# One PSUM pair or two single banks for the VectorE share of the softmax exponential

## The chip, the core and the metric

The kernel runs on one core of one Trainium2 chip. The metric is the device time of one execution in microseconds (us). Five engines work side by side, each with its own queue of instructions in a fixed order: TensorE (PE in the profile; PEld is its weight loading), VectorE (DVE), ScalarE (ACT), GpSimd (POOL) and SyncE (SP, which here only issues DMAs). They meet through semaphores. TensorE writes its products to PSUM, which has eight banks of 512 float32 columns on 128 partitions.

## The reference

```python
xn = layernorm(x)                                   # x: 2048 x 640
q, k, v = split(xn @ wqkv)                          # 32 heads of 20 columns
p = softmax(q @ k.T / sqrt(20))                     # 32 heads, 2048 x 2048 each
s = (p @ v, heads side by side) @ wo
u = gelu(layernorm(xn).T @ w1 + b1)                 # mixes over tokens: 640 x 1536
g = silu((u @ w2 + b2).T)
out = x + s * g
```

The scores are 32 x 2048 x 2048 numbers, and every one goes through an exponential. That is most of the element-wise work of the kernel.

## The kernel before, in words

**Units.** The scores are cut into 2048 units of 128 keys x 512 queries, one PSUM bank each. A unit is one head `g` of a group `G` of four heads, one stretch `p` of 512 queries and one block `c` of 128 keys. The 64 units of one `G` and one `p` make a pass; there are 32 passes. A unit's score product contracts over 32 rows only (20 of them used), so four of them, one for each head of the group, fit side by side in the array (`emit_st`, L910). After the exponential the unit is multiplied with v (`emit_pv`, L1015), which adds up all units of a pass in one accumulator bank, 6. At the end of a pass VectorE reads that bank out and normalises it (`ep_steps`: transpose L1036, reciprocal L1042, product L1047, transpose back L1049), which marks the passes in a trace.

**Two engines take exponentials.** ScalarE owns two pairs of banks, `ACT_GROUPS = ((0, 1), (2, 3))`, and does a pair with one `activation` of 128 x 1024 (L935), in turn. VectorE owns one pair, `DVE_GROUPS = ((4, 5),)`. It has no exponential and makes one out of six steps over the bits of the score (`start_dchain`, N is 512 times the banks in the group):

```python
(tensor_scalar(w3, lo, 0x7FFF, None, ALU.bitwise_and), ...)          # L974, reads PSUM
(tensor_scalar(v_, w_, 1.0 / 256.0, -128.0, ALU.mult, ALU.add), ...) # L975
(tensor_scalar(l_, w_, a3 / 65536.0, ..., ALU.mult, ALU.add), ...)   # L977
(tensor_tensor(l_, v_, l_, ALU.mult), ...)                           # L979
(tensor_tensor(l_, l_, w_, ALU.mult), ...)                           # L980
(scalar_tensor_tensor(o_, zr, ..., l_, ALU.add, ALU.add), ...)       # L981, reads PSUM again
```

The steps need the score on top of a constant, so TensorE first fills each VectorE bank with a product of constants (`prime`, L1313), and the score product is added to it (`start=not dvex` in `emit_st`). A VectorE bank thus goes round: filled with the constant (L1313), score added (L910), L974 to L981, free. The work tiles `ew_sb`, `ev_sb`, `el_sb` exist once; one chain of six runs at a time (`dchain`). The results go to `dpt_sb`, six slots of 512 columns; ScalarE's go to `pt_sb`, 24 slots.

**The order.** All queues are written out beforehand by a planner (`schedule`). It keeps a clock for each engine with prices of its own (VectorE: `dv(n, rate)` = 75 + n x rate ns; ScalarE's pair: 919 ns), and at each step takes the earliest possible candidate, by priority where several are ready. On TensorE a score group for ScalarE has priority 0, v products 1 when many wait, priming 3, a VectorE score group by itself 4; `do_st` puts a primed VectorE group behind a ScalarE group in the same go when its bank is ready. On VectorE a chain step has the lowest priority (90), so other steps stand between those of a chain. No VectorE unit is taken among the last ten units of a pass (`DVE_TAIL_GUARD = 10`, in `dve_room`). On the chip the queues run in this order whatever the true durations are: a TensorE instruction that waits holds all behind it.

**What else runs.** The projections of the next group (L590, evicted by L869 and L865 on VectorE) and the token mixer (L666, evicted by L674; L688 to L704 on VectorE, tanh on ScalarE) are spread over the passes as filler work for TensorE, up to unit 1800 of 2048 (`PACE_TO`). After that come the output projection (L728, L744) and, where the planner wants TensorE busier, products of constants that nobody reads (`warm_step`, L1398); it counts matmul columns in windows of 3413 ns (`_Gate`), a 32-row product as a quarter.

Of the kernel before, what the change touches and what calls it, by code (L numbers as in the profile page):

```python
# [277 lines left out]
class _Kern:  # L278
# [8 lines left out]
    DMAB = 330.0  # L287
    VB = 724
    ACT_GROUPS = ((0, 1), (2, 3))
    DVE_GROUPS = ((4, 5),)  # L290
    ACC_BANK = 6
    DPT = 6
    DVE_EXP = True
# [31 lines left out]
    def build(self):  # L325
# [4 lines left out]
        with es:  # L330
# [4 lines left out]
            def sb(name, shape, d):  # L335
                t[name] = E(nc.sbuf_tensor(name, shape, d))
# [14 lines left out]
            sb("wrm_sb", [P, P + 512], bf)  # L351
            nd = max([len(g) for g in self.DVE_GROUPS] + [0]) * 512 or 2
            sb("ew_sb", [P, nd], u16)
# [26 lines left out]
    def schedule(self):  # L380
# [497 lines left out]
        grp_state = {g: "free" for g in self.ACT_GROUPS}  # L878
        dgrp_state = {g: "free" for g in self.DVE_GROUPS}
        ptr = [0]  # L880
# [337 lines left out]
        act_banks = [b for g in self.ACT_GROUPS for b in g]  # L1218
        dve_banks = [b for g in self.DVE_GROUPS for b in g]
        freebanks.extend([7, 5, 4, 3, 2, 1, 0])  # L1220
# [10 lines left out]
        def fin_bank(b):  # L1231
            return b not in busybanks

        def pe_cands(T):
# [19 lines left out]
            if dveready[0] and self.DVE_EXP:  # L1254
                for dg in self.DVE_GROUPS:
                    if dgrp_state[dg] == "free" and all(fin_bank(b) for b in dg) and nxt[0] + self.DVE_TAIL_GUARD < NU:
# [48 lines left out]
        def dve_room(n):  # L1305
            u0 = nxt[0]
            return (u0 + n <= NU and (u0 % UP) + n <= UP - self.DVE_TAIL_GUARD
                    and all(unit_ok(u0 + i) for i in range(n)))
# [20 lines left out]
        def do_st(grp, us):  # L1329
# [7 lines left out]
            if self.DVE_EXP and dveready[0]:  # L1337
                for dg in self.DVE_GROUPS:
                    if dgrp_state[dg] == "primed" and len(us) + len(dg) <= 4 and dve_room(len(dg)) \
# [152 lines left out]
```

## Time and profile before

| | |
|---|---|
| runs before | 940.67, 945.41, 930.22 us (median 940.67) |
| the profiled execution | 940.67 us, its span 938.9 us |
| busy | TensorE 841.6, VectorE 766.6, ScalarE 866.3 us |
| mean granted TensorE clock | 0.952 |
| ScalarE pairs (L935) | 903, so 1806 of 2048 units |
| VectorE pairs (L974 to L981) | 121, so 242 units |
| VectorE idle before L974 | 118.3 us |
| DMA | 32 GB/s over the span |

The span runs from the first to the last instruction. A row of a group gives the line in the kernel, the engine, output and input tiles with their shapes, the count, the busy time in us and the mean duration of one in ns, then the idle time of that engine just before these instructions and what ended it. The means of ScalarE overlap: one L935 lasts 1064 ns, but 903 of them are busy for 845.6 us, so one starts every 936 ns.

### The profile page before, as it was taken

What the parts mean: (1) busy time and instruction counts of PE and PEld (TensorE: products, weight loads), DVE (VectorE), ACT (ScalarE), POOL (GpSimd) and SP (SyncE); (2) the same over time, 40 slices, a digit from 0 to 9 for tenths busy, and PEclk for the clock granted to TensorE, in tenths of its full rate; (3) what the DMA queues carried; (4) which work ended last, traced back from release to release, by engine and by line L of the source; (5) the groups of instructions that cost most, each with busy time, mean ns of one, the idle gap of its engine ahead of it and who ended that gap; (6) DMA issues with size and microseconds to landing.
All of it is one profiled execution on the core that took longest, in us unless ns stands there. A gap on an engine that the chain in (4) does not pass through costs nothing.

```text
span 938.9 us, 15354 instructions
## 1 busy us (share of the span) xinstructions
PE 841.6 (90%) x5858; PEld 250.5 (27%) x5955; DVE 766.6 (82%) x1255; ACT 866.3 (92%) x942; POOL 13.4 (1%) x31
## 2 busy tenths in 40 slices
PE   6898988998899989889889989989899898899997
PEld 3432222222222222222222222222222223112123
DVE  6878879888878898887888888988888888666577
ACT  2889999999999999999999999999999999878783
POOL 1310000000000000000000000000000000000000
PEclk9999999999999999999999999999999999757569
DMA  8030000000101010100020101101011003400001
GB/s 243 10 97 1 6 7 6 7 6 7 51 1 51 7 51 6 51 7 1 6 74 6 40 8 40 40 2 40 17 30 40 6 7 96 121 1 1 29 29 57
DMA packets 42200, 30.67 MB, mean 33 GB/s; under 512 B 4707, under 2 KB 41571, under 8 KB 42131
## 3 DMA queue, kind: packets, MB, share of 16 engines
q1 hardware_dynamic: 42131, 29.70, 10.6%
q8 instruction: 49, 0.80, 0.4%
q14 instruction: 20, 0.16, 0.1%
HBM read 23.40 MB, written 6.29 MB: 32 GB/s over the span
## 4 chain that ended last, share of the span: by engine, by line
ACT 35%; PE 32%; DVE 25%; issue 4%; DMA 2%; POOL 1%; SPq 0%; DVEq 0%
ACT pt_sb L935 34%; PE ps_all L910 12%; DVE ew_sb L974 7%; PE ps_all L1015 5%; PE ps_all L1313 5%; PE ps_all L666 4%; DVE dpt_sb L981 3%; DVE el_sb L979 3%; PE ps_all L728 3%; DVE el_sb L980 2%; PE ps_all L590 2%; DVE el_sb L977 2%; DVE ev_sb L975 2%; DMA wv_sb<-in_A_wqkv_dram 1%; PE ps_all L609 1%
## 5 line engine op out<-in xcount | busy, mean ns | idle before, releaser
L935 ACT ACTIVATE pt_sb<-ps_all 128x1024 bf16<-128x1024 f32 x903 | 845.6, 1064 | 38.3 <-PE ps_all L910 35.5
L910 PE MATMUL ps_all<-qk_sb 32*128 32x512 bf16 x2048 | 364.6, 400 | 43.5 <-ACT pt_sb L935 32.0
L974 DVE TENSOR_SCALAR ew_sb<-ps_all 128x1024 uint16<-128x1024 uint16 x121 | 148.1, 1224 | 118.3 <-PE ps_all L910 118.2
L910 PEld LDWEIGHTS ps_all<-qk_sb 32*128 32x128 bf16 x2048 | 87.7, 91 | 361.0 <-ACT pt_sb L935 271.0
L1015 PE MATMUL ps_all<-pt_sb,v_sb 128*32 128x512 bf16 x1806 | 169.1, 402 | 0.2 <-ACT pt_sb L935 0.2
L981 DVE SCALAR_TENSOR_TENSOR dpt_sb<-ps_all,el_sb 128x1024 uint16<-128x1024 f32 x121 | 147.8, 1222 | 2.9
L590 PE MATMUL ps_all<-xnT_sb,wqkvp_sb 128*128 128x512 bf16 x289 | 89.5, 386 | 12.3 <-DVE wqk_sb L674 5.6
L979 DVE TENSOR_TENSOR el_sb<-ev_sb,el_sb 128x1024 bf16<-128x1024 bf16 x121 | 83.0, 686 | 2.9
L980 DVE TENSOR_TENSOR el_sb<-el_sb,ew_sb 128x1024 bf16<-128x1024 bf16 x121 | 82.8, 684 | 2.7
L1313 PE MATMUL ps_all<-wrm_sb 128*128 128x512 bf16 x217 | 71.5, 404 | 13.8 <-DVE dpt_sb L981 9.8
L666 PE MATMUL ps_all<-regB,regA 128*128 128x128 bf16 (+1 forms) x369 | 73.9, 299 | 5.6 <-issue 1.7
L666 PE MATMUL ps_all<-regC,regA 128*128 128x512 bf16 (+1 forms) x369 | 71.7, 300 | 4.5 <-DVE qk_sb L869 2.5
L975 DVE TENSOR_SCALAR ev_sb<-ew_sb 128x1024 bf16<-128x1024 uint16 x121 | 50.9, 421 | 3.1
L1015 PEld LDWEIGHTS ps_all<-pt_sb,v_sb 128*32 128x32 bf16 x1806 | 33.7, 95 | 61.9 <-issue 46.7
L977 DVE TENSOR_SCALAR el_sb<-ew_sb 128x1024 bf16<-128x1024 uint16 x121 | 50.2, 415 | 0.0
L1015 PE MATMUL ps_all<-dpt_sb,v_sb 128*32 128x512 bf16 x242 | 49.2, 403 | 0.0
L590 PEld LDWEIGHTS ps_all<-xnT_sb,wqkvp_sb 128*128 128x128 bf16 x320 | 24.1, 97 | 60.4 <-issue 20.8
L609 PE MATMUL ps_all<-wv_sb,xnT_sb 128*128 128x160 bf16 (+1 forms) x160 | 34.5, 313 | 6.4 <-DMA wv_sb<-in_A_wqkv_dram 3.8
L728 PE MATMUL ps_all<-wo_sb,xnT_sb 120*128 120x512 bf16 (+3 forms) x160 | 36.7, 349 | 1.5 <-DVE regC L744 1.3
L666 PEld LDWEIGHTS ps_all<-regB,regA 128*128 128x128 bf16 x384 | 24.8, 97 | 44.1 <-issue 27.7
L666 PEld LDWEIGHTS ps_all<-regC,regA 128*128 128x128 bf16 x384 | 24.8, 97 | 42.8 <-issue 28.6
L869 DVE TENSOR_SCALAR qk_sb<-ps_all,cst_sb 128x512 bf16<-128x512 f32 x32 | 23.7, 742 | 5.7 <-PE ps_all L590 5.3
(69 smaller groups left out, 385.2 us busy)
## 6 DMA issues: line engine op xcount, KB each, us to landing
regA<-in_B_w_dram SPq DMA_DIRECT2D x6, 1024.0 KB, 5.7
regA<-in_B_w_dram SPq DMA_DIRECT2D x8, 768.0 KB
regA<-in_A_x_dram SPq DMA_DIRECT2D x7, 640.0 KB, 4.2
oT_scratch_dram<-stage_sb SPq DMA_DIRECT2D x28, 128.0 KB, 1.8
xnT_sb<-oT_scratch_dram SPq DMA_DIRECT2D x4, 480.0 KB
out_dram<-regC SPq DMA_DIRECT2D x3, 640.0 KB
wqk_sb<-in_A_wqkv_dram SPq DMA_DIRECT2D x2, 800.0 KB
wv_sb<-in_A_wqkv_dram SPq DMA_DIRECT2D x1, 800.0 KB
```

What stands on the lines that cost most here:

```text
L590: steps.append(("pe", lambda e, dc=dc: e.matmul(ps(bk), wqkvp_sb[:, dc, w, G, :], xnT_sb[:, dc, tb * 512:(tb + 1) * 512], start=(dc == 0), ...
L666: steps.append(("pe", lambda e, k=k: e.matmul(ps(bk, n), wap[:, k, col0:col0 + 128], rows[:, k, c0:c0 + n], start=(k == 0), stop=(k == nk ...
L910: pr.pe(lambda e, outp=outp, lhsT=lhsT, rhs=rhs, g=g, dvex=dvex: e.matmul(outp, lhsT, rhs, start=not dvex, stop=True, tile_position=(32 * ...
L935: tk = pr.act(lambda e: e.activation(outp, inp, AF.Exp, scale=math.log(2.0) / 128.0), reads=[bank_slot[b] for b in banks[:n]], writes=[S_( ...
L974: (lambda e: e.tensor_scalar(w3, lo, 0x7FFF, None, ALU.bitwise_and), bs, [S_("ew")], dv(N)),
L975: (lambda e: e.tensor_scalar(v_, w_, 1.0 / 256.0, -128.0, ALU.mult, ALU.add), [S_("ew")], [S_("ev")], dv(N, .26)),
L977: (lambda e: e.tensor_scalar(l_, w_, a3 / 65536.0, (b3 - 64.0 * a3) / 256.0, ALU.mult, ALU.add), [S_("ew")], [S_("el")], dv(N, .26)),
L979: (lambda e: e.tensor_tensor(l_, v_, l_, ALU.mult), [S_("ev"), S_("el")], [S_("el")], dv(N, .52)),
L980: (lambda e: e.tensor_tensor(l_, l_, w_, ALU.mult), [S_("el"), S_("ew")], [S_("el")], dv(N, .52)),
L981: (lambda e: e.scalar_tensor_tensor(o_, zr, -(self.OFFS - 16256.0), l_, ALU.add, ALU.add), bs + [S_("el")], [S_(f"dpt{s0 + i}") for i in r ...
L1015: pr.pe(lambda e, outp=outp, lhsT=lhsT, rhs=rhs, k=k, g=g: e.matmul(outp, lhsT, rhs, start=(k == 0), stop=(k == NB - 1), tile_position=(0, ...
L1313: pe_full(lambda e, b=b: e.matmul(ps(b), wrm_sb[:, 0:P], wrm_sb[:, P:P + 512], start=True, stop=False), [S_("warm"), S_("warm1")], [bank_s ...
```

## The change

One line: VectorE's two banks are no longer a pair but two groups of one bank.

```diff
     ACT_GROUPS = ((0, 1), (2, 3))
-    DVE_GROUPS = ((4, 5),)
+    DVE_GROUPS = ((4,), (5,))
```

Each step of a chain now works on 512 columns instead of 1024, the three work tiles are half as wide, and a chain handles one unit. Each bank is primed and filled by itself, so one can be refilled while the chain of the other runs. The planner lays out all queues anew. Counted in the program that is built: 248 units on VectorE instead of 242 (248 chains of six instead of 121), 900 pairs on ScalarE instead of 903, 248 priming products instead of 242 (nearly all singly, where they stood two by two), 42 products of constants by L1398 instead of 97. VectorE has 2019 instructions instead of 1257. GpSimd's and SyncE's counts are the same. The places of the VectorE units in a pass are typically 0, 1, 8 to 12, 21, 26 to 28, 33 to 35, 40 to 42 and 47 to 49 of 64.

## The prediction

> **What bounds the kernel now.** I read the page's busy shares first, then the costliest groups, then the same groups in the even part of the run, then one chain on the timeline, and last the clock.
>
> ```profile
> PE 841.6 (90%) x5858; PEld 250.5 (27%) x5955; DVE 766.6 (82%) x1255; ACT 866.3 (92%) x942; POOL 13.4 (1%) x31
> L935 ACT ACTIVATE pt_sb<-ps_all 128x1024 bf16<-128x1024 f32 x903 | 845.6, 1064 | 38.3 <-PE ps_all L910 35.5
> L974 DVE TENSOR_SCALAR ew_sb<-ps_all 128x1024 uint16<-128x1024 uint16 x121 | 148.1, 1224 | 118.3 <-PE ps_all L910 118.2
> ```
>
> Three engines are close to full, and ScalarE is fullest. Between 100 and 786 us the group row of L935 says it outright:
>
> ```profile
> L935 ACT ACTIVATE pt_sb<-ps_all 128x1024 bf16<-128x1024 f32 x713 | 664.1, 1068 | 7.9 <-PE ps_all L910 6.0
> ```
>
> ScalarE waits 7.9 us out of 686. There it alone sets the pace, at 0.936 us a pair. VectorE's 118.3 us of idle time before L974 (108 waits on the score product) are the time in which the only pair is primed and filled anew; they cost nothing as long as ScalarE sets the pace. The end of the run is another matter:
>
> ```profile
> PEclk9999999999999999999999999999999999757569
> 84.00:786.00 702.00, 634.74 (x4548) 182.59 (x4627) 595.76 (x922) 692.47 (x757) 0.00 (x0) 1.00 0.07 22
> 808.00:853.00 45.00, 42.00 (x219) 8.77 (x218) 29.78 (x45) 37.20 (x39) 0.00 (x0) 0.62 0.11 34
> 870.00:918.00 48.00, 45.88 (x244) 10.46 (x250) 32.69 (x52) 37.85 (x40) 0.00 (x0) 0.62 0.08 28
> ```
>
> (Columns: stretch, its length, busy us with count of PE, PEld, DVE, ACT, POOL, then granted clock, DMA share, GB/s.) From 808 to 842 and from 859 to 907 us the clock is at half, and TensorE is the full engine. By the marks of L1036, passes 29, 30 and 31 take 32.7, 31.1 and 39.0 us, against 27.1 for the 27 passes before them (731.4 us from 62.1 to 793.5): 21.5 us in all.
>
> **A chain today.** One chain without anything in between:
>
> ```profile
> 319.91 1.23 DVE L974 TENSOR_SCALAR ew_sb<-ps_all 128x1024 uint16<-128x1024 uint16 x1 [0.21 <-PE ps_all L910]
> 321.17 0.43 DVE L975 TENSOR_SCALAR ev_sb<-ew_sb 128x1024 bf16<-128x1024 uint16 x1
> 321.51 0.42 DVE L977 TENSOR_SCALAR el_sb<-ew_sb 128x1024 bf16<-128x1024 uint16 x1
> 321.96 0.69 DVE L979 TENSOR_TENSOR el_sb<-ev_sb,el_sb 128x1024 bf16<-128x1024 bf16 x1
> 322.69 0.69 DVE L980 TENSOR_TENSOR el_sb<-el_sb,ew_sb 128x1024 bf16<-128x1024 bf16 x1
> 323.42 1.22 DVE L981 SCALAR_TENSOR_TENSOR dpt_sb<-ps_all,el_sb 128x1024 uint16<-128x1024 f32 x1
> ```
>
> Starts are 1.26, 0.34, 0.45, 0.73, 0.73 us apart, and L981 lets the next step begin after 1.14 us: 4.65 us a pair. A step that needs the one before starts 0.035 us after its end; one that doesn't starts 0.08 us before it.
>
> **Part 1: VectorE's steps at 512 columns.** No row shows them, so I take them from rows of the same kind at other widths.
>
> ```profile
> L865 DVE CAST qk_sb<-ps_all 128x512 bf16<-128x512 f32 x30 | 20.5, 682 | 4.4 <-PE ps_all L910 3.0 <-PE ps_all L590 1.3
> L702 DVE TENSOR_SCALAR wqk_sb<-wqk_sb 128x640 bf16<-128x640 bf16 x28 | 8.8, 315 | 0.0
> L744 DVE TENSOR_TENSOR regC<-ps_all,regC 128x512 bf16<-128x512 f32 x12 | 8.3, 688 | 8.0 <-PE ps_all L734 4.7 <-PE ps_all L910 3.2
> L692 DVE TENSOR_TENSOR wqk_sb<-wqk_sb 128x640 bf16<-128x640 bf16 x12 | 5.8, 484 | 0.2
> ```
>
> The steps that read PSUM (L974, L981): 1224 ns at 1024, and 682 to 688 ns at 512 in L865 and L744; I take 0.69 us. L975 and L977: 421 at 1024 against 315 at 640 in L702, 0.276 ns a column, so 0.28 us at 512. L979 and L980: 686 at 1024 against 484 at 640 in L692, 0.526 a column, so 0.417 us. With the same spacing: 0.725 + 0.20 + 0.315 + 0.452 + 0.452 + 0.605 = 2.75 us a unit, 5.50 where a pair costs 4.65. The bounds: half of the pair's price, 2.33, if nothing were fixed in a step; and 3.06 if PSUM steps took the 742 ns of L869 and the others the time of the 640-wide rows. I stay at 2.75, since the rows that it lies on are 512 wide or 128 columns off.
>
> Chains: 121 x 4.65 = 563 us become 248 x 2.75 = 682 us, 119 us more work on VectorE, where 118 us of waiting stood. The waiting should go: a bank is refilled (prime 0.32, score 0.4, some 0.2 of latency on each hand-over) within about 1.2 us, while the other bank's chain takes 2.75.
>
> The Trainium skill speaks here on both sides. "Vector Engine (DVE) Microarchitecture Reference", section 5.2, gives about 75 ns for an instruction beside its columns after queue overlap; by that figure a unit is an estimated 2.32 us, VectorE keeps about 3 us spare in a pass, and the change would cost nothing. "VectorE: DVE Perf Modes", in its section on the TRN2 errata, says that a fixed cost is paid once by one large tile and once per tile by many small ones, which speaks against the change; its measured fixed term of about 150 cycles agrees with the 421 ns row (154 ns beyond the columns), and the starts 0.73 us apart for 533 ns of columns show that dependent steps don't overlap.
>
> **Part 2: the two engines in one pass.** I added up the built order, each instruction by its row and spacing, between the marks of L1036, over the same 27 passes. ScalarE: 28 pairs of 0.936 and, once the mixer runs, about one tanh of some 0.6 us: 723.6 us, 26.8 a pass (727.0, 26.9, before; the real 27.1 is 0.6% above it). VectorE: eight units at 2.75 less 0.6 where other steps stand inside a chain, and 5.4 of other steps (normalising, evictions, mixer): 723.8 us, 26.8 a pass, where it had 619.8. So both engines are full at once, and the pass is no longer one engine's sum.
>
> The units on VectorE aren't spread evenly: none stands in the last ten of a pass. From L974 of a pass's first unit to the score product of its last VectorE unit, VectorE has 21.4 us to do (six chains, what stands between, and 1.3 us for the first fill and the last refill), and the 20.6 ScalarE pairs in this stretch need 19.3. From there to the first unit of the next pass there are 7.4 ScalarE pairs and next to no new VectorE unit. If ScalarE stays full, this second stretch takes 6.9 us, and the pass 21.4 + 6.9 = 28.35. If ScalarE has run dry by then, two pairs can be issued at once, and it takes (7.4 - 2) x 0.936 + 0.4 = 5.5: 26.9, no better than either engine's own sum. TensorE's order is fixed, and each priming product waits for L981, with ScalarE's next scores behind it; the planner laid it out for VectorE steps shorter than the rows show, so VectorE will be late at most of these. I take the middle, 27.6: 0.55 us a pass more, for 28 passes at full clock +15 us (from -0.3 to +1.26 a pass: -8 to +35 us).
>
> **Part 3: what costs nothing.** Three ScalarE pairs fewer are 2.8 us less, already in the 26.8. Single priming products: two in a row take 0.54 us of TensorE, two single ones 0.32 each, 124 x 0.1 = 12 us more over the run; TensorE's idle 10% hides it, mainly its waits on L935 before L910 (32 us), and without that cover it adds 0.4 us a pass. `do_st` attaches fewer single units to a ScalarE group, but most still stand right behind one in the order (181 runs of three), so they share its 0.33 us. The 55 products by L1398 that go were filler. The DMAs and SyncE's queue are the same in number, at 32 GB/s.
>
> **Part 4: the end.** Half clock came where TensorE had little to do: just before 808 us it stood idle for 1.4 us waiting for L981. After the filler ends, both orders leave it about as little, so I take the same 21.5 us as now: +0. Bounds: none of it (-21.5), or all of the last four passes at the worst pass's price, 4 x 11.9 - 21.5 = +26. "TensorE: Matmul & The Clock Gate" (section on the HAM clock gate) has the clock come back after one busy window; this trace shows TensorE busy all of 34 us at half clock, so 32-row work seems not to count as busy.
>
> **Sum.** The profiled execution is 940.7 (span 938.9 and 1.8 around it), the median of the three runs. 940.7 + 15 + 0 = 956 us, 1.6% more.
>
> **The rivals.**
> - *Slower: VectorE sets the pace and its end-of-pass gap is added in full.* A pass is 28.35, +1.26 x 28 = +35, so 976 us. For it: priming holds scores in TensorE's fixed order (L981 already holds L1313 for 42 us in total with half as many chains). Against it: ScalarE waits just 7.9 us in the even part in spite of that. It decides from about 27.8 a pass on. With 3.06 us a unit VectorE alone needs 29.3 and the time is 1002.
> - *Faster: the 118 us of waiting go, ScalarE stays full, and the end keeps its clock.* One place, the last four passes: -21.5, and a pass at 26.8, -8, give 911 us; with the clock alone 919. For it: the VectorE work comes in smaller pieces, so TensorE waits shorter for each. Against it: the same lack of filler after unit 1800. It decides only if TensorE never runs short after 800 us, or if a unit costs under 2.6 us and half the cold time goes.
> - *Nothing moves:* VectorE's 118 us are swapped for 119 and ScalarE still sets the pace: 940 us. It lies within the likeliest case's bounds.
>
> **How the numbers follow.** Two per cent, about what a measurement of this kernel can tell from no change, is 922 to 959.5. Balanced engines, 938 to 966 with 956 likeliest: 0.55. The slow rival: 0.28. The fast one: 0.08. Nothing: 0.09. The likeliest case crosses 959.5 in three parts of ten, so slower is 0.28 + 0.17 = 0.45, faster 0.08, within 0.47. The range leaves out the fast rival and the top of the slow one: 930 to 986.
>
> **What would show it.** VectorE busy near 890 us; the 512-wide L974 and L981 near 690 ns, L975 280, L979 417; idle before L974 under 40 us; passes of 27.6 us by the marks of L1036; ScalarE's idle before L935 in the even part up from 7.9 to 20 or more, ended by L910 behind a priming product. It is wrong if the steps come out below 2.6 or above 2.9 us a unit, if L974 still waits 100 us, or if the half-clock time differs from 82 us by more than 30.

## The result, and the profile after

The changed kernel takes 999.65 us in the median of four runs, the kernel before 937.61 us in its four: the ratio is 1.066, with a 95% interval of 1.053 to 1.079. The profiled execution took 1000.6 us, its span 998.7. The forecast was 956, with 930 to 986 as the range: the sign was right, the size was not. Times here and below are medians of all executions, while a ratio compares only the fast ones, those at the higher granted clock, with fast ones of the kernel before that were taken alongside.

The page of the changed kernel: busy shares, the granted clock over the span, the engines on the chain of work that ended last, and the groups of ScalarE's exponential, of the first chain step and of the priming product, its weight load (PEld) and the product itself (PE).

```profile
PE 877.3 (88%) x5804; PEld 262.5 (26%) x5906; DVE 866.5 (87%) x2017; ACT 877.9 (88%) x939; POOL 13.4 (1%) x31
PEclk9999999999979799979989998579999999985599
DVE 48%; PE 29%; issue 12%; ACT 7%; DMA 4%; POOL 1%; SPq 0%; DVEq 0%
L935 ACT ACTIVATE pt_sb<-ps_all 128x1024 bf16<-128x1024 f32 x900 | 854.8, 1038 | 81.6 <-PE ps_all L910 76.8
L974 DVE TENSOR_SCALAR ew_sb<-ps_all 128x512 uint16<-128x512 uint16 x248 | 168.2, 678 | 52.7 <-PE ps_all L910 52.4
L1313 PEld LDWEIGHTS ps_all<-wrm_sb 128*128 128x128 bf16 x248 | 24.1, 98 | 123.4 <-DVE dpt_sb L981 108.9
L1313 PE MATMUL ps_all<-wrm_sb 128*128 128x512 bf16 x214 | 89.2, 418 | 44.1 <-DVE dpt_sb L981 40.8
```

The chain and the rows of L1313 of the kernel before:

```profile
ACT 35%; PE 32%; DVE 25%; issue 4%; DMA 2%; POOL 1%; SPq 0%; DVEq 0%
L1313 PEld LDWEIGHTS ps_all<-wrm_sb 128*128 128x128 bf16 x242 | 14.3, 98 | 41.1 <-DVE dpt_sb L981 32.1 <-issue 5.7 <-DVE regC L744 0.9
L1313 PE MATMUL ps_all<-wrm_sb 128*128 128x512 bf16 x217 | 71.5, 404 | 13.8 <-DVE dpt_sb L981 9.8
```

Three things are new. VectorE's wait before L974 has fallen by 66 us, as meant, but ScalarE now waits 81.6 us before L935 where it waited 38.3. TensorE stands at L1313 for L981: 108.9 us at the weight load, against 32.1 before. The product's own row shows the part of the same waits in which the array had run dry as well, 40.8 us against 9.8; the two rows overlap and don't add up. And the chain that ended last, where ScalarE had 35%, now runs through VectorE for 48% and ScalarE for 7%. The clock row has dents in the middle, where the row before had none until the end.

One chain of the changed kernel on the timeline, up to the start of the next:

```profile
727.37 0.68 DVE L974 TENSOR_SCALAR ew_sb<-ps_all 128x512 uint16<-128x512 uint16 x1
728.09 0.29 DVE L975 TENSOR_SCALAR ev_sb<-ew_sb 128x512 bf16<-128x512 uint16 x1
728.30 0.28 DVE L977 TENSOR_SCALAR el_sb<-ew_sb 128x512 bf16<-128x512 uint16 x1
728.62 0.42 DVE L979 TENSOR_TENSOR el_sb<-ev_sb,el_sb 128x512 bf16<-128x512 bf16 x1
729.08 0.43 DVE L980 TENSOR_TENSOR el_sb<-el_sb,ew_sb 128x512 bf16<-128x512 bf16 x1
729.54 0.69 DVE L981 SCALAR_TENSOR_TENSOR dpt_sb<-ps_all,el_sb 128x512 uint16<-128x512 f32 x1
730.15 0.68 DVE L974 TENSOR_SCALAR ew_sb<-ps_all 128x512 uint16<-128x512 uint16 x1
```

No bracket with idle time stands before the last line: the other bank was full and VectorE went straight on. A unit costs 730.15 - 727.37 = 2.78 us, two of them 5.56 where the pair cost 4.65.

Now the busy times in three stretches: one in the middle in which the clock was at half for about half of the time, the longest one at full clock, and the end (columns as in the prediction).

```profile
571.00:664.00 93.00, 85.99 (x474) 22.12 (x481) 71.37 (x163) 74.80 (x79) 0.00 (x0) 0.74 0.07 22
664.00:892.00 228.00, 198.56 (x1407) 60.14 (x1431) 205.84 (x475) 217.69 (x236) 0.00 (x0) 1.00 0.10 31
892.00:951.00 59.00, 56.09 (x260) 12.43 (x265) 41.32 (x95) 43.64 (x44) 0.00 (x0) 0.51 0.15 48
```

**Where the 60 us are.** The marks of L1036 give the length of each pass, and the clock says which passes it disturbed. The 32 marks before and after, with the start of the first and the last one:

```profile
L1036 DVE STREAM_TRANSPOSE tr_sb<-ps_all x32: 705/707/717, 62.1 to 924.7; 128x512 f32<-128x512 f32 x32
L1036 DVE STREAM_TRANSPOSE tr_sb<-ps_all x32: 705/706/718, 61.9 to 982.4; 128x512 f32<-128x512 f32 x32
```

The 31 passes between them take 862.6 us before and 920.5 after. A pass at full clock lasts 28.24 us on the mean of 20, against 27.09 on the mean of 26 before: 1.15 x 31 = 36 us. The eleven passes touched by half clock (over the whole run there are 160 us of it, before 92) cost 45.1 us beyond that, against 22.9 before: 22 us. The stretch after the last pass is 2 us longer. 36 + 22 + 2 = 60, which is 998.7 - 938.9. Two causes had to be explained: the longer pass, and the clock.

### The profile page after: what moved, and what is told of

The parts are those of the page before. It is cut to its first block, busy times and chain, and to the rows that moved or that the text cites. A ratio compares the mean times of both kernels' runs of the same rounds, so it can differ in the third digit from the quotient of the medians.

```text
span 998.7 us, 16119 instructions
## 1 busy us (share of the span) xinstructions
PE 877.3 (88%) x5804; PEld 262.5 (26%) x5906; DVE 866.5 (87%) x2017; ACT 877.9 (88%) x939; POOL 13.4 (1%) x31
## 4 chain that ended last, share of the span: by engine, by line
DVE 48%; PE 29%; issue 12%; ACT 7%; DMA 4%; POOL 1%; SPq 0%; DVEq 0%
DVE ew_sb L974 11%; PE ps_all L910 10%; DVE el_sb L979 7%; DVE el_sb L980 7%; ACT pt_sb L935 6%; PE ps_all L1015 6%; DVE ev_sb L975 4%; PE ps_all L666 4%; DVE el_sb L977 4%; DMA xnT_sb<-oT_scratch_dram 3%; DVE dpt_sb L981 3%; PE ps_all L1313 3%; PE ps_all L590 3%; PE ps_all L728 2%; DVE wqk_sb L674 2%
## 5 line engine op out<-in xcount | busy, mean ns | idle before, releaser
L935 ACT ACTIVATE pt_sb<-ps_all 128x1024 bf16<-128x1024 f32 x900 | 854.8, 1038 | 81.6 <-PE ps_all L910 76.8
L974 DVE TENSOR_SCALAR ew_sb<-ps_all 128x512 uint16<-128x512 uint16 x248 | 168.2, 678 | 52.7 <-PE ps_all L910 52.4
L981 DVE SCALAR_TENSOR_TENSOR dpt_sb<-ps_all,el_sb 128x512 uint16<-128x512 f32 x248 | 171.0, 690 | 7.6
L1313 PE MATMUL ps_all<-wrm_sb 128*128 128x512 bf16 x214 | 89.2, 418 | 44.1 <-DVE dpt_sb L981 40.8
L979 DVE TENSOR_TENSOR el_sb<-ev_sb,el_sb 128x512 bf16<-128x512 bf16 x248 | 105.2, 424 | 7.8
L980 DVE TENSOR_TENSOR el_sb<-el_sb,ew_sb 128x512 bf16<-128x512 bf16 x248 | 105.1, 424 | 7.8
L1015 PE MATMUL ps_all<-dpt_sb,v_sb 128*32 128x512 bf16 x248 | 96.9, 418 | 0.0
L666 PE MATMUL ps_all<-regC,regA 128*128 128x128 bf16 (+1 forms) x368 | 77.1, 313 | 5.2 <-DVE wqk_sb L674 1.5
L975 DVE TENSOR_SCALAR ev_sb<-ew_sb 128x512 bf16<-128x512 uint16 x248 | 71.7, 289 | 5.6
L977 DVE TENSOR_SCALAR el_sb<-ew_sb 128x512 bf16<-128x512 uint16 x248 | 70.8, 286 | 0.0
L1313 PEld LDWEIGHTS ps_all<-wrm_sb 128*128 128x128 bf16 x248 | 24.1, 98 | 123.4 <-DVE dpt_sb L981 108.9
L666 PEld LDWEIGHTS ps_all<-regB,regA 128*128 128x128 bf16 x384 | 26.6, 100 | 50.0 <-issue 29.1
L728 PE MATMUL ps_all<-wo_sb,xnT_sb 120*128 120x128 bf16 (+3 forms) x160 | 36.4, 344 | 3.7 <-DVE regC L744 2.1
```

The source lines that it names most:

```text
L666: steps.append(("pe", lambda e, k=k: e.matmul(ps(bk, n), wap[:, k, col0:col0 + 128], rows[:, k, c0:c0 + n], start=(k == 0), stop=(k == nk ...
L935: tk = pr.act(lambda e: e.activation(outp, inp, AF.Exp, scale=math.log(2.0) / 128.0), reads=[bank_slot[b] for b in banks[:n]], writes=[S_( ...
L974: (lambda e: e.tensor_scalar(w3, lo, 0x7FFF, None, ALU.bitwise_and), bs, [S_("ew")], dv(N)),
L975: (lambda e: e.tensor_scalar(v_, w_, 1.0 / 256.0, -128.0, ALU.mult, ALU.add), [S_("ew")], [S_("ev")], dv(N, .26)),
L977: (lambda e: e.tensor_scalar(l_, w_, a3 / 65536.0, (b3 - 64.0 * a3) / 256.0, ALU.mult, ALU.add), [S_("ew")], [S_("el")], dv(N, .26)),
L979: (lambda e: e.tensor_tensor(l_, v_, l_, ALU.mult), [S_("ev"), S_("el")], [S_("el")], dv(N, .52)),
```

## The experiments

The theory: VectorE's steps last longer than the planner's prices say (2.78 us a unit, where `dv` adds up to 2.31, or 2.47 with the 40 ns that the planner puts behind each of the four steps that the next one needs), so the order asks VectorE for more than it can do in the first fifty places of a pass; TensorE's fixed queue waits for it, mostly at L1313, and ScalarE's scores wait behind; a TensorE that waits does less work, and the clock falls. The rivals: TensorE's finer order (single priming products) costs by itself; or the clock falls because 42 products of constants are left of 97; or VectorE simply has too much to do in all, which the runs with fewer units bear on further below. Lengths of passes below are means at full clock in the profiled execution, found as above.

**A shorter chain in the same order.** The last two product steps work on 64 of 512 columns.

```diff
-                (lambda e: e.tensor_tensor(l_, v_, l_, ALU.mult), ...
-                (lambda e: e.tensor_tensor(l_, l_, w_, ALU.mult), ...
+                (lambda e: e.tensor_tensor(l_[:, 0:64], v_[:, 0:64], l_[:, 0:64], ALU.mult), ...
+                (lambda e: e.tensor_tensor(l_[:, 0:64], l_[:, 0:64], w_[:, 0:64], ALU.mult), ...
```

> The order of all queues is that of the changed kernel; L979 and L980 work on 64 of a unit's 512 columns (that part of the exponential is left out), so a unit costs VectorE about 2.77 - 2 x 0.235 = 2.30 us. Theory (VectorE is too slow for the order, holds TensorE at L1313 and so ScalarE; the low clock follows from it): VectorE has 23.1 us of work in a pass, ScalarE sets the pace again, passes near 27.1 us, TensorE's waits at L1313 for L981 fall from 150 us to under 60, no half clock in the middle of the run; 915 to 945 us. Rival, TensorE's finer order (single priming products, more changes of mode) is what costs: 980 or more, since TensorE's instructions are the same. Rival, the missing filler products (42 for 97) let the clock fall by themselves: half clock in the middle stays, 970 or more.

Measured: 912.45 us, 0.983 of the kernel before (0.974 to 0.992). A pass is 26.29 us, and half clock comes only at the end. Its waits at L1313 and before L935 in the view of the waits:

```profile
ACT pt_sb L935 <- PE ps_all L910: 21.4, 32, 3.3
PEld ps_all L1313 <- DVE dpt_sb L981: 4.0, 17, 0.4
```

TensorE's queue is the same, instruction for instruction; with a chain no longer than it was priced (a unit with nothing in between costs 2.31 us), the 109 us of waiting for L981 become 4, and the whole loss is gone. Both of the first two rivals fall as causes by themselves: the finer order and the 42 filler products are still there.

**More TensorE work in the same order.** Each priming product is done twice.

```diff
-   pe_full(lambda e, b=b: e.matmul(ps(b), ..., start=True, stop=False), ...)
+   def twice(e, b=b):
+       e.matmul(ps(b), ..., start=True, stop=True)
+       return e.matmul(ps(b), ..., start=True, stop=False)
+   pe_full(twice, ...)
```

> The order is that of the changed kernel; each priming product is done twice in a row, the second over the first, so TensorE has 248 more full products (0.215 us each, 53 us in all) and each 3.4 us window more work. Theory: the clock stays full nearly all the time, passes are 28.5 us everywhere instead of up to 37, since VectorE still sets the pace: 999 - 42 = 957, between 948 and 970. Rival, the clock is the whole cause: about 938. Rival, TensorE is short of time: over 1000.

Measured: 963.79 us, 1.041 of before (1.033 to 1.049), a pass of 28.51. The clock row of its page, in tenths of full speed:

```profile
PEclk8999999999999999999999999999999999999998
```

Of half clock 16 us are left, at both ends. By the lengths of its passes, half clock cost the changed kernel 45 us in the profiled execution; here it costs next to nothing, but a pass is 0.27 us longer, 8 us in all, and the spans differ by 36 us. What is left above the kernel before is the longer pass. Most of the 53 us of extra products disappear in TensorE's waiting.

The same edit in the kernel before:

> The kernel before in its own order, each priming product done twice in a row (242 more full products). It asks what the low clock at the end costs. If too little full-array work after unit 1800 lets the clock fall, the last passes come down from 31 to 39 us to about 28, and the time from 938 to 915 to 925 us. If the clock has another cause, or 52 us more on TensorE is not hidden: 938 to 960.

Measured: 971.28 us, 1.049 of before (1.040 to 1.057). The clock did stay (23 us of half clock), and yet a pass went from 27.09 to 28.51 us. I had not expected that. The wait before L974, by the waits:

```profile
DVE ew_sb L974 <- PE ps_all L910: 155.6, 114, 2.9
```

It was 118.2. With one pair, priming stands between one chain and the next, so 0.43 us more for each of 121 pairs goes onto VectorE's path. It shows up in the pass, and I read it so that VectorE's round of chain and refill was on the critical path of the kernel before already. That TensorE itself was short of time isn't excluded, but as much extra work costs single banks only 0.27 us a pass (above) and 0.43 (below), not 1.42.

**The right prices.** The changed kernel, laid out with the chain as long as it is.

```diff
+            own = ((680., 205., 275., 420., 420., 605.) if n == 1 else (1220., 335., 410., 690., 690., 1140.))
+            ch = [x[:3] + (c,) for x, c in zip(ch, own)]
             dchain.extend((x, us, s0, grp) for x in ch)
```

(With it, and in the runs below but the one with half chains, no bank is primed for the last 24 units, so that none is left over.)

> The changed kernel, laid out with chain steps priced as the traces show them (0.68, 0.205, 0.275, 0.42, 0.42, 0.605 us for 512 columns; 2.77 a unit with the planner's own 40 ns after a step that the next needs). The planner then takes 236 units on VectorE instead of 248 and 906 pairs on ScalarE. Theory: VectorE has about 25.1 us of work in a pass and ScalarE 27.1, L1313 stands where its bank is really free, waits there fall under 80 us, passes near 27.3, the low clock mostly gone from the middle: 935 to 955 us. Rival, single banks cost by TensorE's finer order: 980 or more.

Measured: a pass of 26.51 us, shorter than the 27.3 that were expected, and waits for L981 at the priming product of 26.7 us (weight load) and 4.8 (the product itself). The time doesn't follow: four runs between 921.8 and 956.3 us, with mean granted clocks of 0.979 to 0.932 in the same order, so no ratio can be given. The median is 946.16. In the profiled execution one stretch of 61 us at half clock, right after the start, makes two passes 38 us long. So the longer pass is gone with the right prices; why the clock falls in one execution and not in another, this run doesn't say. (It also gives VectorE 5% fewer units; that fewer units alone don't shorten the pass is shown below.)

With each priming product done twice on top:

> Single banks with true chain prices as in the run before this one of that kind (236 units on VectorE), and each priming product done twice, so that the clock stays. Theory: no stretch of half clock but at the start, passes of about 26.7 us all the way, 62 + 31 x 26.7 + 18 = 908, between 898 and 920 us. Rival, TensorE can't take 51 us more work: 940 or more.

Measured: 929.82 us, 1.006 of before (1.002 to 1.010), all ten runs within 5 us of each other, clock 0.987 to 0.992. That is above the 898 to 920 that were expected. A pass is 26.94. The clock holds but for 17 us late in the run, which cost 13 us; TensorE's extra work costs 0.4 us a pass.

And the pair with the right prices:

> The kernel before (one pair), laid out with the chain priced as its trace shows it (1.22, 0.335, 0.41, 0.69, 0.69, 1.14 us). The planner takes 110 pairs on VectorE instead of 121, and 914 pairs on ScalarE instead of 903. Theory (the wrong prices cost the kernel before something too: ScalarE's pairs can follow each other every 0.903 us, but a pass took 27.1 us where 28.2 x 0.903 + 0.6 is 26.1): passes of about 26.6 us, 915 to 930 us unless the clock falls more often. Rival, the kernel before was held by ScalarE alone: 11 pairs more are 10 us more, 940 to 948.

Measured: 912.11 us, 0.985 of before (0.977 to 0.994), the best that was run with the whole computation. A pass is 26.88, a little less than 27.09; the larger part is the clock, 0.991 to 0.997, with 127 products of constants where there were 97: passes 29 to 31 take 79.1 us together, not 102.8. The expected 26.6 was missed.

**The smaller step without the second bank.** The pair stays, and its chain runs in two halves.

```diff
+            ...     # half(k): the six steps on columns k*512 to k*512+511
+            ch = [(f,) + x[1:3] + (x[3] / 2 - 20.0,) for k in range(2) for f, x in zip(half(k), ch)]
             dchain.extend((x, us, s0, grp) for x in ch)
```

> The kernel before keeps its pair of banks, primed and filled together, but the chain runs in two halves of 512 columns, one after the other (twelve steps; each priced at half its step less 20 ns, so that the order stays close: 117 pairs on VectorE instead of 121, 907 on ScalarE). This is the change's smaller step without its second bank. Theory (a unit of 512 columns costs 2.77 us where half a pair cost 2.33, and that is what hurts): 3.66 x (5.53 + 1.0) + 4.8 = 28.7 us a pass where VectorE has 27 now, so 970 to 1005 us with the lower clock that follows. Rival (two groups in TensorE's order hurt, not the step): 925 to 945.

Measured: 1055.94 us, 1.135 of before (1.119 to 1.152), a pass of 30.34 where 28.7 was expected. So without the second bank the smaller step makes a pass some 3.2 us longer, and the changed kernel, which has that bank, stands 2.1 below it (30.34 against 28.24). These aren't clean shares of the two halves of the change: the planner priced a pair here at 4.18 - 0.24 = 3.94 us beside its 40 ns, where two single units are priced at 4.63, so VectorE is further behind the order than in the changed kernel, and it has 234 units instead of 248.

**Where the units stand.** Five runs with the planner's own low prices. First eight units a pass, spread out (the diff leaves out where `in_pass` is set up, and where `take_dve` counts in it; where units are spread, `DVE_TAIL_GUARD` is 8 in `dve_room`):

```diff
         def dve_room(n):
             u0 = nxt[0]
+            if u0 // UP != in_pass[0]:
+                in_pass[:] = [u0 // UP, 0]
+            if u0 % UP < int(7.5 * in_pass[1]):
+                return False
```

> The changed kernel with its own too low prices, but VectorE's eight units of a pass are taken no earlier than at places 0, 7, 15, 22, 30, 37, 45 and 52 of 64 (246 units in all, so VectorE has the same 26.9 us of work in a pass). Theory: the 1.6 us a pass in which VectorE stands idle at the end of a pass goes, and TensorE waits less at L1313 within it: passes near 27.3 instead of 28.5, the low clock less often: 945 to 970 us. Rival, VectorE's total work is all that counts: passes stay at 28.5, 985 to 1005.

Measured: 970.95 us, 1.039 of before (1.024 to 1.055), a pass of 28.19 in the mean, 27.99 in the median, against 28.24 and 28.45 in the changed kernel: by the mean next to nothing of the 1.2 us that were expected, by the median less than half. Then seven a pass, at their old places (`if in_pass[1] >= 7: return False`):

> The changed kernel with its own prices, but at most seven units a pass on VectorE (216 in all, 916 pairs on ScalarE). Theory: VectorE has 6.75 x 2.69 + 5.4 = 23.6 us of work in a pass and no longer holds ScalarE, which needs 28.6 x 0.903 + 0.6 = 26.5; passes of 26.6 to 27.2, half clock at the end alone: 910 to 945 us. Rival, single banks cost by their finer order on TensorE: passes stay above 28, over 965.

Measured: 1014.93 us, 1.100 of before (1.087 to 1.114), a pass of 28.39. This is the miss that taught most: VectorE has 13% fewer units, is busy for 785 us instead of 866, and the pass is no shorter. VectorE's total work is not what sets it, which is the last of the rivals. Then the same seven spread out (8.8 in place of 7.5):

> As the run with seven units a pass (216 on VectorE, 916 pairs on ScalarE, the changed kernel's own prices), but the units are taken no earlier than at places 0, 8, 17, 26, 35, 44 and 52 of 64, where that run had them at 0, 1, 10, 21, 28, 35 and 42. The planner puts in 143 products of constants where that run had 54. Revised theory (what counts is whether VectorE can follow the order locally: between units 7 places apart ScalarE needs 3 x 0.903 = 2.7 us and VectorE 2.7 for the chain and some 0.7 for what stands between; 9 places apart ScalarE needs 3.6, and VectorE follows): passes near 26.8 at full clock, ScalarE's waits before L935 under 40 us, 900 to 940 us. Rival (single banks with the planner's low prices are slow wherever their units stand): 28.5 a pass, over 960.

Measured: 962.41 us, 1.028 of before (1.016 to 1.040). In the profiled execution, 947.06 us, the clock never fell, but a pass is 28.19, near the rival's 28.5. That contradicts the theory as revised there: units nine places apart leave VectorE time, and it waits 92 us before L974. The waits, and the row of the clock:

```profile
PEld ps_all L1319 <- DVE dpt_sb L981: 94.8, 187, 1.9
DVE ew_sb L974 <- PE ps_all L910: 92.3, 86, 3.0
ACT pt_sb L935 <- PE ps_all L910: 27.6, 82, 1.8
PEclk9999999999999999999999999999999999999999
```

(L1319 is the priming product here.) As I read it, TensorE waits for VectorE at a product that nobody needs for some microseconds, because the order has it where the chain was thought to end. Priming moved 1.0 us later (`pr.ready(...) + 1000.0` in its candidate):

> The run with seven evenly placed units a pass (216 on VectorE, 916 pairs), with one thing more: the planner may place a priming product only 1.0 us after the time at which it thinks the bank free. Products of constants by L1398: 118. Theory after that run (its VectorE has work for 24 of 28.4 us and ScalarE for 26.4, and yet both wait: TensorE stands at L1313, placed where the planner's too low prices end the chain, 0.3 to 1 us before L981 really ends, and ScalarE's scores stand behind it, while nobody needs the primed bank for another 2 to 4 us): waits at L1313 fall from 132 us to under 40, passes from 28.4 to about 27, 905 to 935 us. Rival (VectorE, or TensorE's finer order, holds the pass by itself): 28 a pass, 945 to 965.

Measured: a pass of 27.20 us, with next to no waiting for L981 at L1319, so the waiting there was worth 1.0 us a pass.

```profile
PEld ps_all L1319 <- DVE dpt_sb L981: 2.4, 7, 0.6
PEclk9999999999999899989997999999999889975557
```

The time is 952.48 us, 1.020 of before (1.005 to 1.035), above the 905 to 935 that were expected: there are 147 us of half clock in the profiled execution, the slowest of the four, with 118 products of constants where 143 had been. The two rows of the clock also speak against half of my theory: with 95 us of waiting at the priming product the clock never fell, and with 2 us it fell for 147. So that waiting isn't by itself what brings half clock. The same late priming in the changed kernel:

> The changed kernel with its own low prices, each priming product placed no earlier than 1.0 us after the planned end of its chain. The planner then takes 244 units on VectorE instead of 248, 902 pairs on ScalarE. Theory: 7.6 x 2.69 + 5.4 = 25.9 us of VectorE work in a pass, waits at L1313 from 150 us to under 90 (VectorE's lag of 0.3 us a unit adds up over the first fifty units, so 1 us doesn't cover it all), passes about 27.4, the low clock rarer: 930 to 965 us. Rival (VectorE's work, not where the priming stands): 28.2 a pass and 975 to 1000.

Measured: 1003.63 us, 1.074 of before (1.059 to 1.090), a pass of 27.95, near the rival's numbers. The waits at L1313 are down and little is won, as the waits of TensorE's weight loads show:

```profile
PEld ps_all L590 <- DVE wqk_sb L674: 17.7, 24, 1.5
PEld ps_all L1015 <- DVE dpt_sb L981: 16.9, 34, 1.2
...
PEld ps_all L1313 <- DVE dpt_sb L981: 11.4, 29, 0.8
```

TensorE now waits for VectorE elsewhere: at a projection whose bank the mixer's eviction frees late (L674; 7.8 us in the changed kernel), and at the v products (none there). I take it that with eight early units VectorE is late for everything, and L1313 is only where it showed first.

**What is shown and what isn't.** That the chain being longer than the order allows makes the pass longer is shown from both ends: shorten the chain (26.29) or lengthen its price (26.51), and 28.24 is gone. That waiting at L1313 carries some of it is shown for seven even units alone. Why seven units at their old places don't shorten the pass is argued, not shown: as in the prediction's second part, VectorE sets the pace up to the last unit and ScalarE alone after it, and with the last unit at place 42 instead of 49 the second stretch is only longer. The two runs with units spread out, in which no such second stretch should be left, still had passes of 28.19, so this can't be all of it. What lets the clock fall in one execution and not in the next is open. More work on TensorE keeps it up (16 us of half clock for 160), and in the changed kernel it fell behind stretches with little of it: its records change in steps of 3.41 us, and counting a 32-row or 32-column product as a quarter of its columns, the nine such steps before a fall (after 60 us) hold 2176 to 3360 columns, while nine in ten of the 216 at full clock after which it stayed full hold 3520 or more. That is my count from the traces, not an experiment.

## Why the prediction was wrong, point by point

- *A unit at 2.75 us* (part 1): 2.78. Right, and the bank is mostly filled in time, though L974 still waits 52.7 us where it was to be under 40. VectorE busy: 866 for "near 890", which the sum of overlapping durations had too high.
- *The pass at 27.6* (part 2): 28.24. This is the first step that failed, and it was a choice: of the two ends, 26.9 and 28.35, I took the middle, and the measured pass lies at the upper one, the slow rival's. The prediction named what did the damage, VectorE steps longer than the planner's and priming products that wait for L981 with ScalarE's scores behind them, but took half of it as given back. ScalarE did run dry, as its 81.6 us of waiting say; that it would catch up by two pairs at the end of a pass no run shows. Instead of +15 us it was +36. (The 42 us for which L981 held L1313 before are 32.1 and 9.8 added up, and nearly all of the 9.8 lies within the 32.1.)
- *What stood behind that choice* was a reading: ScalarE waits 7.9 us in 686, so it alone sets the pace, at 0.936 us a pair, and VectorE's idle time costs nothing. Group L935 alone, between 100 and 600 us, in the kernel before, with the shortened chain, and in the changed kernel (busy us and count, clock, DMA share, GB/s):

```profile
100.00:600.00 500.00, 483.97 (x520) 1.00 0.07 21
```

```profile
100.00:600.00 500.00, 492.93 (x535) 1.00 0.07 21
```

```profile
100.00:600.00 500.00, 455.43 (x483) 0.95 0.06 19
```

  With 520 pairs alone ScalarE was 97% busy (98.5% with its tanh), and it could do 535. A pair lasts 1.04 to 1.12 us in the groups, but in the trace its start can follow the last one after 0.903; one that comes 0.1 us late shows no idle time at all. So busy was not full, and the 0.936 us a pair held waiting. ScalarE's own sum in a pass is 28 x 0.903 + 0.6 = 25.9, not 26.8, so something else was already in play in the kernel before; the doubled priming product points to VectorE (27.09 to 28.51).
- *The clock at +0* (part 4): +22. The second step that failed. I allowed for half clock only after unit 1800, where it had been, though I had written that it came when TensorE waited for L981, and that VectorE would be late at most priming products. The shortened chain, in the same order, has none in the middle, so in this order VectorE's lateness brought it; how, is open, as said above. (In the 34 us of half clock after 808 us, TensorE was busy for 32.2, not all.)
- *The rivals.* The slow one had VectorE setting the pace, held priming products and the pass (28.35), and stood at 976 us; with the 22 us of the clock it would have been 998. Its other part, a gap at the end of a pass that is added in full, isn't shown: spread units left a pass at 28.19, so the agreement of that sum may be luck. The 55 filler products that go were not the cause, as its own run shows.
- *The skill.* "VectorE: DVE Perf Modes", section on the TRN2 errata, warned against many small tiles, and the trace agrees: 5.56 us for 4.65, though 512 columns just meet the 512 elements a tile that it recommends. The 75 ns of "Vector Engine (DVE) Microarchitecture Reference", section 5.2, hold here for a step that doesn't need the one before (L981 to the next L974: 0.61 us for 533 ns of columns) and not for one that does (L974 to L975: 0.72, which is 190 ns). Four of the six hand-overs in a chain are of the second kind; the planner had priced all as the first, beside 40 ns.

## What to carry to other kernels

An order that is laid out in advance is only as good as its prices: before a change that makes one engine's pieces smaller and more frequent, compare the prices with the trace step by step, dependent and independent hand-overs apart, and mend them first (here that alone took 1.5% off the kernel before, mostly through the clock). A high busy share of an engine whose instructions overlap can hide waiting; count how many it finishes in a stretch, and compare with the closest spacing of two starts. When two engines share the work and a third feeds both from one queue, a wait that frees one can be paid by the other, and where TensorE has little full-width work the clock can add to the bill (22 of the 60 us here).

## What the runs showed of the hardware

TensorE can be busy and stay at half clock: 56.09 of 59 us between 892 and 951 us in the changed kernel, at a clock of 0.51, with mostly 32-row score products and 32-column v products in it (196 of 260 records). "TensorE: Matmul & The Clock Gate", in its part on the HAM clock gate, has full clock return after a busy window of about 3.4 us; these runs don't agree, unless such products count for less than their time. With the 248 repeated priming products, all full-width, half clock all but vanished (16 us for 160). And the clock of one order can differ from execution to execution: with the right prices on single banks, four executions took 921.8 to 956.3 us at mean clocks of 0.979 to 0.932.
